# Two decode attentions in one kernel: how the last keys and the last values are split into transfers, and where the last output weights are reordered

## The chip, the cores and the metric

The kernel runs on one core of one Trainium2 chip. The metric is the device time of one execution in microseconds (us). Three executions of the kernel before took 1374.40, 1374.57 and 1374.70 us; the median is 1374.57.

## What is computed

Two attention layers decode one token for each of four batch rows; their outputs are put side by side. Layer A has 32 query heads that share 8 heads of keys and values, and looks at the last 2048 of 8192 positions. Layer B has 32 heads of its own and looks at all 8192 positions. All tensors are bf16, a head is 128 wide.

```python
def _A_ref(x, k_cache, v_cache, wq, wo):
    ...
    W = min(4096, max(256, Sk // 4))
    q = (x @ wq).reshape(B, Sq, Hq, Dh).transpose(0, 2, 1, 3)
    k = jnp.repeat(k_cache[:, :, Sk - W:, :], rep, axis=1)
    v = jnp.repeat(v_cache[:, :, Sk - W:, :], rep, axis=1)
    ...
def _B_ref(x, k_cache, v_cache, wq, wo):
    B, Sq, D = x.shape
    H, Dh = 32, 128
    q = (x @ wq).reshape(B, Sq, H, Dh).transpose(0, 2, 1, 3)
    scores = jnp.einsum("bhqd,bhkd->bhqk", q, k_cache) * (Dh ** -0.5)
    p = _softmax(scores, axis=-1)
    o = jnp.einsum("bhqk,bhkd->bhqd", p, v_cache)
    return o.transpose(0, 2, 1, 3).reshape(B, Sq, H * Dh) @ wo
...
return jnp.concatenate([a, b], axis=-1)
```

Almost all of the data is the key and value cache of layer B: 4 rows x 32 heads x 8192 positions x 128 x 2 bytes, 268 MB each for keys and values.

## The kernel before

**Chunks.** The caches are worked in chunks. A chunk of layer A is one shared head of all four rows (2 MB of keys, 2 MB of values). A chunk of layer B is two heads of one batch row: 128 tiles of 128 positions, 4 MB of keys and 4 MB of values, with each of the 128 partitions holding one contiguous run of 32 KB. There are 8 chunks of A (`NCA`) and 64 of B, 72 in all (`NC`); the last chunk is `NC - 1`.

**One chunk on the engines.** For each group of eight key tiles (`TG`), TensorE transposes the tiles into PSUM (`emit_T`), VectorE or ScalarE copies the result to SBUF (lines 475 and 477), and two groups later TensorE multiplies the transposed keys by the queries (`emit_S`). That is `keys_part`, 16 groups for a chunk of B. `values_part(c, nxt)` then runs the value product (`emit_pv`) of the chunk before while the softmax of the chunk just scored is worked out (row maximum, maximum over partitions, exponential). The value product of a chunk comes thus one chunk later than its scores. The last chunk has no successor: its value product stands at the end of the program, after line 806, followed by the division (`norm_out`), the output product (`emit_fin`) and the store.

**Order.** Nothing is scheduled automatically. The class `_Sched` records the operations of each engine in the order of the Python code, with the keys that an operation waits for; each key becomes a count of a semaphore, each engine's list is emitted in order, and the repeating part as a hardware loop.

**Loads.** All loads of caches and weights are issued by SyncE (SP) in one list (lines 375 to 398), each as one transfer of 128 partitions, and each waits until the buffer that it fills is free. The tensor `kv` has ten slots of 2 MB; B chunks use four of them for keys and four for values in turns of two, and the last values use slots 8 and 9, which hold layer A's keys earlier and are free early. So the last values can be issued before those of the chunk ahead of them are used. `dma_kv` issues them:

- the last keys in two pieces at lines 369 to 371: the first `LASTK` = 96 of 128 tiles (3 MB), then the other 32 (1 MB), with a semaphore of its own, `d_kl`;
- the last values in five pieces at lines 361 to 365, `LASTV` = 64, 32, 16, 8 and 8 tiles (2 MB, 1 MB, 512 KB, 256 KB, 256 KB), each with its own semaphore, `d_vl0` to `d_vl4`. `emit_pv` waits for a piece at its first tile (line 632).

**How waits for the second piece of the keys are made.** After the issue of the values of each odd chunk of B, SP waits for the output weights of B's current head pair (`wos`), in the last chunk also for `d_kl`, and then raises a count (line 394, keys `wos2`). TensorE waits for that count before the transposes of group `LASTK // TG` = 12 of every odd chunk of B (line 468), and before the output product (line 707), which `keys_part` puts after group 10. The transposes of the last chunk's group 12 so never start before the second piece of the keys is there.

**The last output weights.** `emit_fin` of the other chunks takes its left operand through `emit_sel`, which reorders the attention output. For the last chunk the weights are reordered instead, ahead of time: `emit_wol` (lines 686 to 696) multiplies them by constant selection matrices, four products of 512 columns into the PSUM tensor `tr`, and ScalarE and VectorE copy the two halves to `wol`. It stands after the first piece of the last value product, at line 810:

```python
for g in range(chunks[NC - 1]["NG"]):
    emit_pv(NC - 1, g)
    if g == LASTV[0] // TG - 1:
        emit_wol()
```

Of the kernel before, what the change touches and what calls it, by code (L numbers as in the profile page):

```python
# [12 lines left out]
P = 128  # L13
TG = 8
# [5 lines left out]
NSM = 2  # L20
SLAG = 2
NW = 64
LASTK = 96
LASTV = (64, 32, 16, 8, 8)

TRM0, BC0, L0, Q0, XT0 = 0, 256, 288, 320, 448
# [133 lines left out]
def bass_concat_heads__sliding_block_cached__mha_block_cached__decode_kernel(  # L160
# [31 lines left out]
    NCA = Hkv  # L192
# [8 lines left out]
    NTA, NTB = chunks[0]["NT"], chunks[-1]["NT"]  # L201
# [3 lines left out]
    sch = _Sched()  # L205
    with ExitStack() as es:
# [97 lines left out]
        def take(load, at, n, release):  # L304
            waits = []
            for i in range(at, at + n):
                waits += held[i]
                held[i] = [release]
            half_of[load] = at
            return waits  # L310

        def flat(at, n):
            return kv[:, at:at + n, :].rearrange("p s x -> p (s x)")
# [28 lines left out]
        def dma_kv(kind, c):  # L342
            ch = chunks[c]
            T = {("k", 0): A_k, ("k", 1): B_k, ("v", 0): A_v, ("v", 1): B_v}[(kind, ch["ab"])]

            at = HALF_A[kind][c % 2] if ch["ab"] == 0 else (0 if kind == "k" else 4) + 2 * (c % 2)

            if kind == "v" and c == NC - 1:
                at = 8
            waits = take((kind, c), at, 1 if ch["ab"] == 0 else 2, ("T", ch["s_last"]) if kind == "k" else ("pv", c))  # L350
            if kind == "v" and c == NCA + 1:
                waits = waits + [("pv", NONE)]
            if ch["ab"] == 0:
                src = T[:, ch["g"], SkA - W:, :].rearrange("b (pp j) d -> pp b (j d)", pp=P // NB)
                sch.add_dma("sp", lambda e: e.dma_start(kv[:, at, :], src), "d_h%d" % at, waits=waits, key=(kind, c))
                return
            src = T[ch["b"], 2 * ch["hp"]:2 * ch["hp"] + 2].rearrange("u (pp j) d -> (u pp) (j d)", pp=P // 2)
            dst = flat(at, 2)
            if kind == "v" and c == NC - 1:

                j0 = 0
                for i, n in enumerate(LASTV):
                    x = slice(j0 * P, (j0 + n) * P)
                    sch.add_dma("sp", lambda e, x=x: e.dma_start(dst[:, x], src[:, x]), "d_vl%d" % i, waits=waits, key=("vl", j0))
                    j0 += n
                return
            if kind == "k" and c == NC - 1:

                x = slice(0, LASTK * P), slice(LASTK * P, NTB * P)
                sch.add_dma("sp", lambda e: e.dma_start(dst[:, x[0]], src[:, x[0]]), "d_h%d" % at, waits=waits, key=(kind, c))  # L370
                sch.add_dma("sp", lambda e: e.dma_start(dst[:, x[1]], src[:, x[1]]), "d_kl", key="kl")
                return
            sch.add_dma("sp", lambda e: e.dma_start(dst, src), "d_h%d" % at, waits=waits, key=(kind, c))

        dma_x(0)
        dma_x(1)
        dma_wq(0, 0)
        dma_kv("k", 0)
        dma_wq(1, 6)

# [5 lines left out]
        for kind, c in loads:  # L386
            if kind == "k" and c >= NCA and (c == NCA or (c - NCA) % 4 == 3 and c > NCA + 3):
                dma_wos((c - NCA) // 4)
            dma_kv(kind, c)
            if kind == "v" and c > NCA and (c - NCA) % 2 == 1:  # L390


                hp = max(0, c - NCA - 2) // 4
                sch.add("sp", lambda e: e.sem_inc(sems["eng_sp"], 1), waits=[("wos", hp)] + (["kl"] if c == NC - 1 else []),
                        key=("wos2", c - 2 if c > NCA + 1 else NONE), self_inc=True)
            if kind == "v" and c < NCA:
                dma_wo(c)
# [7 lines left out]
        def pe_mm(o, l, r, start=True, stop=True, transpose=False, waits=(), key=None):  # L405
            if transpose:
                sch.add("pe", lambda e: e.transpose(o, l, r), waits, key)  # L407
            else:
                sch.add("pe", lambda e: e.matmul(o, l, r, start=start, stop=stop), waits, key)  # L409
# [37 lines left out]
        def tile_of(kind, c, j):  # L447
            at = half_of[(kind, c)]
            return flat(at, chunks[c]["NT"] // NTA)[:, j * P:(j + 1) * P]

        def ahead(c, n):

            return c - n if c - n >= NCA else NONE
# [3 lines left out]
        def emit_T(s):  # L457
            c, g = groups[s]
            bank = g % NTRB
            if c == NCA and g == 0:  # L460
                bank_used[:] = [None] * NTRB
            before, bank_used[bank] = bank_used[bank], s
            for t in range(TG):
                waits = []
                if t == 0:
                    waits = [("k", c), "c_identb"] if g == 0 else []
                    waits += [("ev", before)] if before is not None else []
                    if c >= NCA and c % 2 == 1 and g == LASTK // TG:
                        waits += [("wos2", ahead(c, 2))]
                pe_mm(tr[:, bank, t * P:(t + 1) * P], tile_of("k", c, g * TG + t), identb[:, :], transpose=True,  # L470
                      waits=waits, key=("T", s) if t == TG - 1 else None)
            src, dst = tr[:, bank, :], kt[:, s % NKT, :]
            waits = [("T", s)] + ([("S", s - NKT)] if s >= NKT else [])
            if (g % 3 == 2) if c >= NCA else (g in (0, 1, 3, 5)):
                sch.add("act", lambda e: e.activation(dst, src, ACTF.Copy), waits=waits, key=("ev", s))  # L475
            else:
                sch.add("dve", lambda e: e.tensor_copy(dst, src), waits=waits, key=("ev", s))  # L477
# [36 lines left out]
        def bcast(ap, dims):  # L514
            return bass.AP(ap.tensor, ap.offset, [ap.ap[0]] + dims)
# [122 lines left out]
        def norm_sum(c):  # L638
            if 0 <= c < NCA:
                m, n, rs, ri = c % NSM, 16, rst[0][:, c % NSM, :], rinv[:, c % NSM, :]  # L640
            else:
                m, n, rs, ri = NSM, 4, rst[1][:, :], rinv[:, 0, 0:4]
            pe_mm(ms[:, L0:L0 + n], onesf[:, :], rs, waits=([("rs", c), "c_onesf"] if c != NONE else []) + ms_read, key=("L", c))
            sch.add("dve", lambda e: e.reciprocal(out=ri, in_=ms[:, L0:L0 + n]), waits=[("L", c)], key=("rinv", c))
            if c >= NCA or c == NONE:

                pair = 4 * (c - NCA - 1 + 4) if c != NONE else 8
                pv = pm[:, :, :, :, :].rearrange("p a b c d -> p (a b c d)")
                sch.add("dve", lambda e, x=0: e.tensor_tensor(
                    out=rz[:, :].rearrange("p (x y) -> p x y", x=2), in0=bcast(ri, [[0, 2], [1, 4]]),  # L650
                    in1=pv[:, bass.ds(x + pair, 8)].rearrange("p (x y) -> p x y", x=2), op=ALU.mult),
                    waits=[("rinv", c), "c_pm"], key=("rz", c), at=pair)
            ms_read[:] = [("rinv", c)]
            rs_read[m] = [("L", c)]
# [31 lines left out]
        def emit_wol():  # L686

            for u in range(2):
                o = tr[:, u, :].bitcast(F32)
                for r in range(2):  # L690
                    pe_mm(o, back2[:, u, r, :], wos[:, r, :], start=r == 0, stop=r == 1,
                          waits=[("wos2", NC - 1)] if u == r == 0 else [], key=("back", u) if r else None)
                if u == 0:
                    sch.add("act", lambda e, o=o: e.activation(wol[:, 0, :], o, ACTF.Copy), waits=[("back", 0)], key=("wol", 0))
                else:
                    sch.add("dve", lambda e, o=o: e.tensor_copy(wol[:, 1, :], o), waits=[("back", 1)], key=("wol", 1))
# [26 lines left out]
        def pv_done(c):  # L723
            if c < NCA or (c - NCA) % 2:
                norm_out(c)
# [79 lines left out]
            values_part(None if c == 0 else NONE if c == NCA else c - 1, c)  # L805
        sch.mark()
        norm_sum(NC - 1)
        for g in range(chunks[NC - 1]["NG"]):
            emit_pv(NC - 1, g)
            if g == LASTV[0] // TG - 1:  # L810
                emit_wol()
        pv_done(NC - 1)
        emit_fin(NC - 1)

# [58 lines left out]
```

## Time and profile before

| what | value |
|---|---|
| time of the profiled execution | 1374.7 us |
| its span, first to last instruction | 1372.9 us |
| median of three runs | 1374.57 us |
| TensorE busy (PE) | 1181.3 us, 86% |
| its weight loads (PEld) | 1131.3 us, 82% |
| VectorE (DVE) | 657.2 us, 48% |
| ScalarE (ACT) | 434.8 us, 32% |
| mean granted TensorE clock | 0.939 |
| bytes read from HBM | 587.21 MB |
| keys of B, 63 loads of 4 MB | 27.1 us median from issue to landing |
| values of B, 63 loads of 4 MB | 31.4 us |
| last keys, 3 MB and 1 MB | 24.4 and 26.5 us |
| last values, 2 MB, 1 MB, 512 KB, 2 x 256 KB | 35.8, 37.8, 38.6, 38.7 us |

The engine names are those of the profile: PE is TensorE's matmul, PEld its weight load, SPq the instruction queue of SyncE, which issues the loads. L409 and L407 are the lines of one helper, `pe_mm`, through which all matmuls and transposes go, so they are told apart by their tiles: `tr<-identb,kv` are the transposes of keys, `sc<-qb,kt` the scores, `po<-pbb,kv` the value product, `tr<-wos,back` the reordering of the last output weights, `fin<-wol,oz` the last output product. "idle before <- releaser" behind an instruction tells how long its engine stood still and what ended that. "DMA share" is the mean busy share of the core's 16 DMA engines. A transfer's time from issue to landing includes the time that it lies behind earlier ones.

### The profile page before, as it was taken

What the parts mean: (1) busy time and instruction counts of PE and PEld (TensorE: products, weight loads), DVE (VectorE), ACT (ScalarE), POOL (GpSimd) and SP (SyncE); (2) the same over time, 40 slices, a digit from 0 to 9 for tenths busy, and PEclk for the clock granted to TensorE, in tenths of its full rate; (3) what the DMA queues carried; (4) which work ended last, traced back from release to release, by engine and by line L of the source; (5) the groups of instructions that cost most, each with busy time, mean ns of one, the idle gap of its engine ahead of it and who ended that gap; (6) DMA issues with size and microseconds to landing.
All of it is one profiled execution on the core that took longest, in us unless ns stands there. A gap on an engine that the chain in (4) does not pass through costs nothing.

```text
span 1372.9 us, 59836 instructions
## 1 busy us (share of the span) xinstructions
PE 1181.3 (86%) x27001; PEld 1131.3 (82%) x27001; DVE 657.2 (48%) x1434; ACT 434.8 (32%) x650; POOL 7.3 (1%) x28
## 2 busy tenths in 40 slices
PE   4898899888888988888899888888898888888988
PEld 4777898888888988888888878887888888888987
DVE  1775455444444544444445444444454444444544
ACT  1553233233233332333233323322333233223332
POOL 2000000000000000000000000000000000000000
PEclk9998999999999999999999999999999999999999
DMA  9999999999999999999999999999999999999998
GB/s 400 422 426 431 428 432 430 433 431 433 431 433 431 431 432 431 433 430 433 430 433 430 430 432 434 428 433 430 433 430 432 432 432 432 430 433 429 434 427 348
DMA packets 25253, 587.53 MB, mean 428 GB/s; under 512 B 2816, under 2 KB 2832, under 8 KB 6288
## 3 DMA queue, kind: packets, MB, share of 16 engines
q1 hardware_dynamic: 25208, 587.22, 99.7%
q8 instruction: 16, 0.26, 0.1%
q14 instruction: 5, 0.04, 0.0%
q10 hardware_dynamic: 24, 0.01, 0.0%
HBM read 587.21 MB, written 0.01 MB: 428 GB/s over the span
## 4 chain that ended last, share of the span: by engine, by line
DMA 59%; PE 37%; DVE 1%; issue 1%; ACT 1%; SPq 0%; DVEq 0%
DMA kv<-in_B_k_cache_dram 53%; PE tr L407 23%; PE sc L409 9%; DMA kv<-in_B_v_cache_dram 3%; PE po L409 2%; DMA kv<-in_B_wq_dram 2%; PE fin L409 2%; DMA kv<-in_A_k_cache_dram 1%; PE ms L409 1%; DVE sA L526 1%; ACT kt L475 0%; ACT pba L596 0%; DVE rm L535 0%; DVE sA L524 0%; PE ms L407 0%
## 5 line engine op out<-in xcount | busy, mean ns | idle before, releaser
L407 PE MATMUL tr<-identb,kv 128*128 128x128 bf16 x8704 | 697.4, 230 | 144.2 <-DMA kv<-in_B_k_cache_dram 139.5
L477 DVE COPY kt<-tr 128x1024 bf16<-128x1024 bf16 x736 | 502.9, 691 | 460.0 <-PE tr L407 455.6
L407 PEld LDWEIGHTS tr<-identb,kv 128*128 128x128 bf16 x8704 | 553.0, 104 | 166.9 <-DMA kv<-in_B_k_cache_dram 105.8
L475 ACT ACTIVATE kt<-tr 128x1024 bf16<-128x1024 bf16 x352 | 359.3, 1023 | 668.6 <-PE tr L407 668.3
L409 PE MATMUL sc<-qb,kt 128*128 128x64 bf16 x8704 | 444.8, 196 | 13.4 <-ACT kt L475 12.8
L409 PEld LDWEIGHTS sc<-qb,kt 128*128 128x128 bf16 x8704 | 364.9, 100 | 24.1 <-ACT kt L475 20.3
L409 PE MATMUL po<-pbb,kv 128*128 128x64 bf16 x8320 | 284.5, 192 | 5.3 <-issue 4.9
L409 PEld LDWEIGHTS po<-pbb,kv 128*128 128x128 bf16 x8320 | 263.3, 97 | 7.9 <-issue 5.1
L576 ACT ACTIVATE pbb<-sc,negb 64x128 bf16<-64x128 f32 x128 | 51.5, 403 | 252.4 <-DVE negb L563 251.6
L540 DVE TENSOR_REDUCE rm<-sc 64x1 f32<-64x128 f32 x128 | 37.0, 289 | 55.8 <-PE sc L409 55.0
L552 DVE TENSOR_REDUCE gm<-ms 1x2 f32<-1x128 f32 (+1 forms) x72 | 20.1, 279 | 47.8 <-PE ms L407 47.8
L563 DVE COPY negb<-ms 128x1 f32<-128x1 f32 (+1 forms) x72 | 11.4, 159 | 47.0 <-PE ms L409 47.0
L409 PE MATMUL ms<-identf,gx 1*128 1x1 f32 (+1 forms) x144 | 27.4, 257 | 0.8 <-DVE zA L682 0.8
L409 PEld LDWEIGHTS ms<-identf,gx 1*128 1x128 f32 (+1 forms) x144 | 21.3, 184 | 4.7 <-DVE zA L682 0.9
L665 DVE TENSOR_TENSOR oz<-po,rz 128x8 bf16<-128x8 f32 x33 | 5.5, 167 | 40.4 <-PE po L409 40.4
L576 ACT ACTIVATION_READ_ACCUMULATOR pbb<-sc,negb 64x1 f32 x128 | 23.7, 185 | 0.0
L407 PE MATMUL ms<-identf,rm 128*1 128x128 f32 (+1 forms) x72 | 19.6, 272 | 3.8 <-DVE rm L535 3.8
L409 PE MATMUL po<-pba,kv 128*128 128x64 bf16 x512 | 20.5, 199 | 2.6 <-ACT pba L596 1.4
L409 PEld LDWEIGHTS po<-pba,kv 128*128 128x128 bf16 x512 | 17.9, 102 | 5.4 <-ACT pba L596 4.2
L409 PE MATMUL fin<-wos,zB 128*4 128x512 bf16 x64 | 19.0, 378 | 0.0
L556 DVE TENSOR_SCALAR gx<-gm 1x128 f32<-1x128 f32 (+1 forms) x72 | 15.9, 221 | 2.5
L682 DVE CAST zB<-ms 64x8 bf16<-64x8 f32 x64 | 10.5, 164 | 8.9 <-PE ms L409 8.5
(61 smaller groups left out, 169.7 us busy)
## 6 DMA issues: line engine op xcount, KB each, us to landing
kv<-in_B_k_cache_dram SPq DMA_DIRECT2D x63, 4096.0 KB, 27.1
kv<-in_B_v_cache_dram SPq DMA_DIRECT2D x63, 4096.0 KB, 31.4
kv<-in_A_k_cache_dram SPq DMA_DIRECT2D x8, 2048.0 KB, 13.6
kv<-in_A_v_cache_dram SPq DMA_DIRECT2D x8, 2048.0 KB, 15.4
kv<-in_A_wq_dram SPq DMA_DIRECT2D x1, 4096.0 KB, 12.3
kv<-in_B_wq_dram SPq DMA_DIRECT2D x1, 4096.0 KB, 27.1
wor<-in_A_wo_dram SPq DMA_DIRECT2D x8, 512.0 KB, 9.5
wos<-in_B_wo_dram SPq DMA_DIRECT2D x16, 256.0 KB, 20.4
```

The costliest lines, as they stand in the source:

```text
L407: sch.add("pe", lambda e: e.transpose(o, l, r), waits, key)
L409: sch.add("pe", lambda e: e.matmul(o, l, r, start=start, stop=stop), waits, key)
L475: sch.add("act", lambda e: e.activation(dst, src, ACTF.Copy), waits=waits, key=("ev", s))
L477: sch.add("dve", lambda e: e.tensor_copy(dst, src), waits=waits, key=("ev", s))
L526: emit = lambda e, src=src, b=b: e.scalar_tensor_tensor(out=t, in0=src, scalar=mk[:, b:b + 1], in1=t, op0=ALU.mult, op1=ALU.add)
L540: sch.add("dve", lambda e, src=src, pp=pp: e.tensor_reduce(out=rm[pp, m, 0:1], in_=src, axis=AX.X, op=ALU.max), waits=[("S", ch["s_last"]) ...
L552: sch.add("dve", lambda e: e.tensor_reduce(out=gm[0:C, m, 0:U], in_=src, axis=AX.X, op=ALU.max), waits=[("trm", c)], key=("gmax", c))
L556: sch.add("dve", lambda e: e.tensor_scalar(out=dst, in0=gv, scalar1=-scale, scalar2=None, op0=ALU.mult), waits=[("gmax", c)], key=("gx", c))
L563: sch.add("dve", lambda e: e.tensor_copy(negb[:, m, 0:C], ms[:, col:col + C]), waits=[("bc", c)], key=("negb", c))
L576: sch.add("act", lambda e, src=src, pp=pp, n=n, u=u: e.activation(probs_of(c)[pp, :, u], src, ACTF.Exp, bias=negb[pp, m, 0:1], scale=scale ...
L665: sch.add("dve", lambda e: e.tensor_tensor(out=o, in0=i0, in1=i1, op=ALU.mult), waits=waits, key=("oT", c))
L682: sch.add("dve", lambda e, src=src, pp=pp: e.tensor_copy(z[pp, :].rearrange("p (r b) -> p r b", r=k), src), waits=[("sm", c)] + free if h ...
```

## The change

Three things change, all for the last chunk but for the position of one wait:

- the last keys come in two halves of 2 MB (64 tiles each), and the wait on the count of line 468 moves from group 12 to group 8 in every odd chunk of B; `LASTK` is gone;
- the four products and two copies of `emit_wol` are issued ahead of the last value product and not within it;
- the first 2 MB piece of the last values, one transfer of 128 partitions, becomes five transfers on the same semaphore: partitions 96 to 103, 104 to 111, 112 to 119 and 120 to 127, eight partitions of 16 KB each (128 KB a transfer), and then partitions 0 to 95 (1.5 MB). The key that the value product waits for is the count after all five.

The bytes loaded and the arithmetic are the same.

```diff
-LASTK = 96
 LASTV = (64, 32, 16, 8, 8)
...
                 for i, n in enumerate(LASTV):
                     x = slice(j0 * P, (j0 + n) * P)
-                    sch.add_dma("sp", lambda e, x=x: e.dma_start(dst[:, x], src[:, x]), "d_vl%d" % i, waits=waits, key=("vl", j0))
+                    if i == 0:
+
+                        for y in [slice(96 + 8 * k, 104 + 8 * k) for k in range(4)]:
+                            sch.add_dma("sp", lambda e, x=x, y=y: e.dma_start(dst[y, x], src[y, x]), "d_vl%d" % i, waits=waits)
+                        sch.add_dma("sp", lambda e, x=x: e.dma_start(dst[0:96, x], src[0:96, x]), "d_vl%d" % i, waits=waits, key=("vl", j0))
+                    else:
+                        sch.add_dma("sp", lambda e, x=x: e.dma_start(dst[:, x], src[:, x]), "d_vl%d" % i, waits=waits, key=("vl", j0))
                     j0 += n
                 return
             if kind == "k" and c == NC - 1:
 
-                x = slice(0, LASTK * P), slice(LASTK * P, NTB * P)
+                x = slice(0, NTB // 2 * P), slice(NTB // 2 * P, NTB * P)
...
-                    if c >= NCA and c % 2 == 1 and g == LASTK // TG:
+                    if c >= NCA and c % 2 == 1 and g == NTB // TG // 2:
                         waits += [("wos2", ahead(c, 2))]
...
         norm_sum(NC - 1)
+        emit_wol()
         for g in range(chunks[NC - 1]["NG"]):
             emit_pv(NC - 1, g)
-            if g == LASTV[0] // TG - 1:
-                emit_wol()
         pv_done(NC - 1)
```

## The prediction, made before the changed kernel ran

> **What bounds the kernel now.** I read the page's table of slices first, then its queue table, then the end of the chain of waits, then the timeline and the busy windows of the last 30 us. The profiled execution took 1374.7 us: a span of 1372.9 and 1.8 around it. The median of the runs shown, 1374.57, is 0.13 lower; the sum below is made against 1374.7.
>
> ```profile
> DMA  9999999999999999999999999999999999999998
> HBM read 587.21 MB, written 0.01 MB: 428 GB/s over the span
> q1 hardware_dynamic: 25208, 587.22, 99.7%
> q10 hardware_dynamic: 24, 0.01, 0.0%
> ```
>
> The load queue is busy 99.7% of the span. 428 GB/s over 16 engines is 26.8 GB/s for each, so a row of 16 KB takes 16384 / 26.8 = 0.61 us. The packet counts tell how transfers are split. The kernel issues 175 loads of 128 partitions and one store of four rows on q1: 175 x (128 + 16) + (4 + 4) = 25208, that is one packet a row and one small completion packet for each of 16 engines. On q10 there are three transfers of four rows, and 3 x (4 + 4) = 24: four rows go to four engines.
>
> ```profile
> 1330.42 38.58 DMA kv<-in_B_v_cache_dram
> 1369.04 0.42 PE po L409 x8
> 1369.56 0.18 DVE oz L665
> 1369.78 0.61 PE fin L409 x2
> 1370.41 0.68 DVE outsb L717
> ```
>
> The chain ends on the landing of the fifth piece of the last values at 1369.0; behind it lies a fixed tail of 3.9 us of span (eight tiles, the division, the output product, the store). What ends the program is when the slowest DMA engine has written its last row.
>
> ```profile
> core 0: us, PE busy (x) PEld busy (x) DVE busy (x) ACT busy (x) POOL busy (x), PEclk, DMA share, GB/s
> 1360.00:1365.00 5.00, 5.00 (x151) 4.87 (x148) 1.58 (x7) 0.91 (x4) 0.00 (x0) 1.00 0.98 405
> 1365.00:1366.00 1.00, 1.00 (x39) 1.00 (x35) 0.00 (x0) 0.00 (x0) 0.00 (x0) 1.00 0.67 268
> 1366.00:1367.00 1.00, 1.00 (x15) 0.53 (x12) 0.01 (x1) 0.45 (x1) 0.00 (x0) 1.00 0.56 223
> 1367.00:1368.00 1.00, 1.00 (x39) 1.00 (x36) 0.68 (x1) 0.15 (x1) 0.00 (x0) 1.00 0.52 193
> 1368.00:1369.00 1.00, 0.82 (x23) 0.58 (x18) 0.00 (x0) 0.00 (x0) 0.00 (x0) 1.00 0.11 43
> ```
>
> The DMA share falls from 1365 on: the engines don't end together. The completion packets in the trace's transfer records give it engine by engine (span time): seven end between 1365.4 and 1366.4, two near 1367.2, seven between 1368.6 and 1369.0. The idle shares after 1365 add to 0.33 + 0.44 + 0.48 + 0.89 = 2.1 us, which is all that a perfect spread could give, 0.16%.
>
> **The change, part by part.**
>
> ```profile
> 1328.21 7.75 SPq L364 DMA_DIRECT2D kv<-in_B_v_cache_dram  x5
> 1343.95 1.35 PE L409 MATMUL po<-pbb,kv 128*128 128x64 bf16 x40
> 1346.98 1.51 PE L407 MATMUL tr<-identb,kv 128*128 128x128 bf16 x24 [1.68 <-DMA kv<-in_B_k_cache_dram]
> 1359.15 0.65 PE L409 MATMUL po<-pbb,kv 128*128 128x64 bf16 x16 [0.23 <-DMA kv<-in_B_v_cache_dram]
> 1363.75 0.39 PE L409 MATMUL ms<-rsb,onesf 128*128 128x4 f32 x2
> 1364.04 1.93 PEld L409 LDWEIGHTS po<-pbb,kv 128*128 128x128 bf16 x64
> 1365.92 1.02 PE L409 MATMUL tr<-wos,back 128*128 128x512 bf16 x4
> 1366.78 2.04 PE L409 MATMUL po<-pbb,kv 128*128 128x64 bf16 x56
> ```
>
> *Last keys in halves.* The first piece shrinks from 3 MB, landing at 1346.9, to 2 MB: 1 MB at 428 GB/s is 2.4 us, so it lands at 1344.5. PE is free at 1343.95 + 1.35 = 1345.3, so the transposes start 1.7 us sooner. The second half still lands at 1322.86 + 26.5 = 1349.4, the bytes ahead of it being the same; the ninth group, which waits for it through the SP count, comes at 1352.0 - 1.7 = 1350.3, so no wait. But the values of the chunk before land at 1359.1 as now; PE reaches them at 1357.2, waits 1.9 in place of 0.23, and goes on at 1359.15. Worth 0. The cover is that landing; were it gone, the gain would be 1.7. The earlier wait on the SP count in every odd chunk (group 8 for 12) is met there: the trace has no PE wait on SP at all, and the product after group 10 waits for the same count now; the register instruction that it adds lies under the 139.5 us in which PE waits for keys of the second attention.
>
> *Output weights first.* Four products move from between the first 64 and the other 64 value tiles to ahead of them. They hold PE from 1365.92 to 1366.78, 0.86 us. They now run from 1364.04 to 1364.9, while the first piece is landing or late. PE's work to the end is the same: last eight tiles not before 1364.9 + 120 x 1.93/64 = 1368.5, against 1369.04 now. Worth 0 while the landing is later than that.
>
> *Nine issues for five on SP.* Four more issues at 0.43 us. The fifth of the present ones was held for 5.5 us (to 1336.0) with nine transfers outstanding. Behind them SP has the count that the ninth key group waits for. If the hold goes by rows outstanding, SP is free by 1338, far ahead of the keys at 1349.4. Worth 0; the other case is a rival.
>
> *The first 2 MB of values.* 128 rows in one transfer, eight rows an engine, 8 x 0.61 = 4.9 us, become 96 rows (six an engine) and four transfers of eight rows. By the packet counts an eight-row transfer goes to eight engines, a row each. The trace has none of 16 KB rows, so I bound its time t. Below: eight rows side by side, t = 0.61. Above: sixteen equal streams feed 128 partitions, so eight neighbouring partitions get one stream's worth in all loads of this kernel; if the 26.8 GB/s belongs to what is written into and not to the engine, the eight rows take 8 x 0.61 = 4.9. No row decides, since in the 128-partition loads engine and destination are always paired alike. The nearest is the first load of x, 4 KB into four partitions: in the transfer records its packets ran side by side within 97 ns, where one stream would need 152; that excludes the top for small packets, which may only have been buffered. I take the middle: two streams (four rows deep, 2.44), or one sharer more because the other engines still write there (five deep, 3.05); their mean, t = 2.75.
>
> The eight engines then spend 4t + 6 x 0.61 in place of 8 x 0.61, that is 4t - 1.22 more. If these are the engines that end early (the latest of them at 1367.3), the landing comes at 1367.3 + 4 x 2.75 - 1.22 = 1377.1, 8.1 after 1369.0. Sum: 1374.7 + 0 + 0 + 0 + 8.0 = **1382.7 us**. Four deep gives 1381.5, five deep 1384.0. The engines' order rests on the first four only: in the records the packets of the third four-row transfer lie in four of the eight streams that are ahead at that time (129 us).
>
> [...]
>
> [...]
>
> **The rivals.**
> - *The rows run side by side, on the early engines.* t = 0.61: the early eight end 1.22 later (1368.5 at most), the late ones 1.22 sooner (1367.8). PE then decides with 1368.5: 1374.7 - 0.5 = 1374.2. For it: the x packets, and 2.1 us of idle shares to be had. Against: a rate of 26.8 GB/s an engine that no load exceeds.
> - *The same, on the late engines or with no use:* 1369.0 + 1.22, so 1375.9. Against it: the four-row transfers on early streams.
> - *SP is held by transfers, not rows.* Each new issue waits until an older load is through: the ninth one then waits for the values before, landing until 1359.1, and the count for the ninth group comes at 1356 to 1359 in place of 1350.3. Slack is 1.9 (until 1352.2), then it decides: 4 to 7 us on PE, less about 1 us of waits there: 1377.5 to 1380.5. For it: the 5.5 us hold. Against: it ended at 1336.0, when the load under way was unfinished on nine engines.
> - *All eight rows in line:* t = 4.88, landing 1367.3 + 18.3 = 1385.6, so 1391.3.
>
> **How the numbers follow.** Shared writes, two to six deep (t 1.22 to 3.66; 1375.4 to 1386.4): 0.58, its own likely range 1378 to 1386.5. Side by side on the early engines, 1374.2: 0.24. On the late ones, 1375.9: 0.05. SP held: 0.06. In line: 0.07. 0.2% is 2.75 us, about what a measurement of this kernel can tell from no change. Faster by that is beyond the 2.1 us that idle engines leave: 0.02 for what I don't see. Within it are the second and third case and a little of the first (below three deep): 0.30. Slower: 0.68. The range, 1374.0 to 1386.0, leaves out the line-up and the ends.
>
> **What would show it.** The queue q1 should count 25208 + 32 = 25240 packets (4 x 16 + 112 for 144). Right, if 16 KB packets last over 1 us in the records where they last 0.61 now, the first piece lands near 1372 and the wait of PE before its first 64 value tiles is several us; the DMA share falls below 0.9 from 1356 on. Wrong, if packets stay at 0.61 and the share keeps above 0.9 until 1367: then it is the first rival. A PE wait at the ninth key group near 1350 would show the SP rival. Transposes of the last keys should start at 1345.3, and the output weights at 1364.0. The step I trust least is t.

## The result, and the profile after

The changed kernel takes 1386.2 us (median of 6 runs, 1385.28 to 1387.62) against 1374.43 for the kernel before (6 runs, 1374.17 to 1374.70): a ratio of 1.0086, 95% interval 1.0073 to 1.0099. It is slower by 11.8 us. The runs also scatter over 2.3 us, where those of the kernel before lie within 0.5. The profiled execution took 1386.49 us with a span of 1384.7.

The first lines are from the page of the changed kernel: its queue table and the table of slices.

```profile
PEclk9998999999999999999999999999999999999997
DMA  9999999999999999999999999999999999999997
GB/s 401 422 424 433 428 430 431 434 429 432 434 432 429 431 434 428 432 434 431 431 432 433 431 431 433 430 431 431 434 430 431 432 431 433 432 431 432 433 430 198
q1 hardware_dynamic: 25240, 587.22, 99.6%
```

The queue counts 25240 packets, 32 more than before, as worked out from eight rows and eight completions for each new transfer. All slices but the last are nearly as before; the last, 34.6 us long, moves 198 GB/s (348 before) while its DMA share still reads 7 tenths.

Next, the busy windows of the changed kernel at its end. The columns are the window, its length, busy time of PE, PEld, DVE, ACT and POOL, the granted clock, the DMA share and GB/s.

```profile
1350.00:1355.00 5.00, 5.00 (x112) 4.51 (x110) 3.31 (x8) 2.05 (x2) 0.00 (x0) 1.00 1.01 423
1355.00:1360.00 5.00, 1.95 (x47) 1.71 (x43) 1.38 (x3) 1.02 (x1) 0.00 (x0) 1.00 1.02 233
1360.00:1365.00 5.00, 2.61 (x49) 2.61 (x50) 0.58 (x2) 0.00 (x0) 0.00 (x0) 0.52 0.95 193
1365.00:1370.00 5.00, 5.00 (x100) 4.44 (x97) 1.00 (x5) 0.96 (x5) 0.00 (x0) 0.80 0.95 200
1370.00:1375.00 5.00, 0.58 (x7) 0.23 (x6) 0.69 (x1) 0.55 (x1) 0.00 (x0) 0.88 0.92 220
1375.00:1380.00 5.00, 5.00 (x99) 5.00 (x97) 0.00 (x0) 0.00 (x0) 0.00 (x0) 0.50 0.29 111
```

This is the reading to learn from. From 1355 to 1375 the DMA engines are busy 92% of the time or more, and they move 193 to 233 GB/s, about half of the 423 just before. The busy share is the time that packets take, so packets that are held up look like work (those of 16 KB took 1.22 us in the mean, 0.61 before); GB/s beside it shows that something is wrong. The clock column falls to 0.52 and 0.50 in the windows that come with PE's waits of 5.24 and 4.42 us.

The timeline of PE in the changed kernel, with the waits that ended there (L412 and L414 are the lines of `pe_mm` here; in the experiments its lines shift by a few):

```profile
1345.22 1.50 PE L412 MATMUL tr<-identb,kv 128*128 128x128 bf16 x24
1350.26 0.61 PE L412 MATMUL tr<-identb,kv 128*128 128x128 bf16 x8
1362.39 1.04 PE L414 MATMUL po<-pbb,kv 128*128 128x64 bf16 x16 [5.24 <-DMA kv<-in_B_v_cache_dram]
1369.32 1.02 PE L414 MATMUL tr<-wos,back 128*128 128x512 bf16 x4
1374.77 6.57 PE L414 MATMUL po<-pbb,kv 128*128 128x64 bf16 x128 [4.42 <-DMA kv<-in_B_v_cache_dram]
```

Transposes of the last keys start at 1345.22 and the ninth group goes at 1350.26 without a wait. The values of the chunk ahead now land at 1362.4, 3.2 us later than in the kernel before (1359.15). The first piece of the last values lands at 1374.7 where PE found it at 1364.04. Then all 128 tiles run in one stretch of 6.57 us with no wait for the four later pieces. The chain of waits of the changed kernel says the same:

```profile
1331.18 43.54 DMA kv<-in_B_v_cache_dram
1374.73 0.04 issue
1374.77 6.58 PE po L414 x128
```

The sum closes: the first piece is 10.7 us later (1374.73 - 1364.04). From there to the end of the value product it takes 6.6 us, where the kernel before took 5.4 (1364.04 to 1369.47): 1.2 more. That is 11.9 us, and the span grew by 11.8. Read from the other end: the last piece lands at 1379.5 in this trace (1369.0 before), 10.5 later, and what follows it takes 5.3 us in place of 3.9, as PE is still busy with earlier tiles.

The transfer records (one line a packet) give the time of a packet, by size, after 1350 us of span. "Added" is the time over the usual one, summed and divided by 16 engines.

| packet | usual | changed kernel, mean | added per engine |
|---|---|---|---|
| 32 KB, values of the chunk ahead | 1.22 us | 1.44 us | 1.30 us |
| 16 KB, first piece | 0.61 us | 1.22 us | 4.87 us |
| 8 KB, second piece | 0.31 us | 0.58 us | 2.15 us |
| 4 KB, third piece | 0.16 us | 0.24 us | 0.63 us |
| 2 KB, fourth and fifth | 0.085 us | 0.10 us | 0.26 us |

Not one of the 128 16 KB packets of the first piece took over 0.622 us in the kernel before. In the changed kernel the slowest took 1.64, and 32 KB packets of the chunk ahead took up to 2.65. Packets of loads that the change doesn't touch are slow too: those of the second piece took 0.58 us in place of 0.31.

### The profile page after: what moved, and what is told of

Same layout as the page of the kernel before. It is cut to its first block, busy times and chain, and to the rows that moved or that the text cites. A ratio compares the mean times of both kernels' runs of the same rounds, so it can differ in the third digit from the quotient of the medians.

```text
span 1384.7 us, 59840 instructions
## 1 busy us (share of the span) xinstructions
PE 1184.2 (86%) x27001; PEld 1133.5 (82%) x27001; DVE 656.6 (47%) x1434; ACT 435.1 (31%) x650; POOL 7.4 (1%) x28
## 3 DMA queue, kind: packets, MB, share of 16 engines
q1 hardware_dynamic: 25240, 587.22, 99.6%
## 4 chain that ended last, share of the span: by engine, by line
DMA 62%; PE 36%; issue 1%; DVE 1%; ACT 1%; SPq 0%; DVEq 0%
DMA kv<-in_B_k_cache_dram 53%; PE tr L412 22%; PE sc L414 9%; DMA kv<-in_B_v_cache_dram 3%; DMA kv<-in_A_k_cache_dram 3%; PE po L414 3%; DMA kv<-in_B_wq_dram 2%; PE fin L414 2%; PE ms L414 1%; ACT kt L480 0%; DVE sA L531 0%; ACT pba L601 0%; PE ms L412 0%; DVE zA L687 0%; SPq L366 0%
## 5 line engine op out<-in xcount | busy, mean ns | idle before, releaser
L412 PE MATMUL tr<-identb,kv 128*128 128x128 bf16 x8704 | 694.1, 230 | 143.3 <-DMA kv<-in_B_k_cache_dram 136.0
L412 PEld LDWEIGHTS tr<-identb,kv 128*128 128x128 bf16 x8704 | 549.3, 104 | 166.1 <-DMA kv<-in_B_k_cache_dram 97.5
L414 PE MATMUL sc<-qb,kt 128*128 128x64 bf16 x8704 | 446.4, 196 | 14.7 <-ACT kt L480 12.8
L414 PEld LDWEIGHTS sc<-qb,kt 128*128 128x128 bf16 x8704 | 366.0, 100 | 26.4 <-ACT kt L480 20.2
L414 PE MATMUL po<-pbb,kv 128*128 128x64 bf16 x8320 | 288.7, 193 | 14.6 <-DMA kv<-in_B_v_cache_dram 9.7
L414 PEld LDWEIGHTS po<-pbb,kv 128*128 128x128 bf16 x8320 | 267.8, 98 | 17.2 <-DMA kv<-in_B_v_cache_dram 10.3
L414 PE MATMUL ms<-identf,gx 1*128 1x1 f32 (+1 forms) x144 | 27.2, 256 | 0.8 <-DVE zA L687 0.8
L414 PEld LDWEIGHTS ms<-identf,gx 1*128 1x128 f32 (+1 forms) x144 | 21.1, 182 | 4.6 <-DVE zA L687 0.9
L414 PE MATMUL po<-pba,kv 128*128 128x64 bf16 x512 | 20.5, 199 | 2.6 <-ACT pba L601 1.4
L414 PEld LDWEIGHTS po<-pba,kv 128*128 128x128 bf16 x512 | 17.9, 102 | 5.4 <-ACT pba L601 4.2
L412 PE MATMUL ms<-identf,rm 128*1 128x128 f32 (+1 forms) x72 | 19.7, 273 | 2.7 <-DVE rm L540 2.7
L414 PE MATMUL fin<-wos,zB 128*4 128x512 bf16 x64 | 19.0, 378 | 0.0
L687 DVE CAST zB<-ms 64x8 bf16<-64x8 f32 x64 | 10.5, 164 | 9.4 <-PE ms L414 8.9
```

The costliest lines, as they stand in the source:

```text
L687: sch.add("dve", lambda e, src=src, pp=pp: e.tensor_copy(z[pp, :].rearrange("p (r b) -> p r b", r=k), src), waits=[("sm", c)] + free if h ...
```

## The experiments

Three theories were held against each other, each a supposition for the runs to test. P: the partitions written decide; a row keeps the usual rate where its engine writes the block of partitions that it writes in a load of 128, and is slow where it meets other engines. (Which partitions an engine writes stands in no record.) S: a transfer of eight rows has a price of its own. B: only the bytes per engine count. A fourth, H, puts the cost on the reading side of memory. Every run was compared with runs of the kernel before on the same chip.

**one_transfer: keys and output weights as changed, no split.**

```diff
-                    if i == 0:
...
+                    sch.add_dma("sp", lambda e, x=x: e.dma_start(dst[:, x], src[:, x]), "d_vl%d" % i, waits=waits, key=("vl", j0))
```

> The changed kernel with the first piece of the last values as one transfer of 128 partitions again; keys in halves and output weights first stay. If the split alone costs (both theories of it): 1374.4 us as before, within 0.5, packets of 16 KB rows at 0.61 us, transposes of the last keys starting about 1.7 us earlier than before against the landing of the values ahead, and PE waiting about 2 us for those. If the keys or the output weights carry part of the cost: 1375 to 1386 us.

Measured: 1374.83 us against 1374.60, ratio 1.0003 (0.9993 to 1.0012). The keys in halves and the moved output weights change nothing that the runs can tell. Its PE timeline shows where the head start goes:

```profile
1345.00 1.50 PE L406 MATMUL tr<-identb,kv 128*128 128x128 bf16 x24
...
1359.01 0.65 PE L408 MATMUL po<-pbb,kv 128*128 128x64 bf16 x16 [2.08 <-DMA kv<-in_B_v_cache_dram]
...
1363.86 1.02 PE L408 MATMUL tr<-wos,back 128*128 128x512 bf16 x4
1364.72 3.94 PE L408 MATMUL po<-pbb,kv 128*128 128x64 bf16 x120
1368.88 0.41 PE L408 MATMUL po<-pbb,kv 128*128 128x64 bf16 x8 [0.23 <-DMA kv<-in_B_v_cache_dram]
```

The transposes start 2.0 us sooner than in the kernel before, and the wait for the values ahead grows from 0.23 to 2.08 us. The output weights fill the time before the first 120 tiles, and the last eight still wait for the landing.

**split_only: the kernel before with nothing but the split.** Its edit is the part of the diff of `dma_kv` that begins with `if i == 0`, put into the kernel before.

> The kernel before with the split of the first piece alone: keys in three and one quarters and output weights within the value product stay. If the split is the whole cost: 1386 us, within the scatter of the changed kernel (1385.3 to 1387.6), perhaps 0.3 to 0.9 us more, as the four products of the output weights then come after the late landing. If keys in halves carry part of it: 1375 to 1384 us.

Measured: 1387.03 us against 1374.49, ratio 1.0090 (1.0073 to 1.0106). With the run before it, the whole cost is in the split.

**rows32_rows96: one transfer of 32 rows in place of four of eight.**

```diff
-                        for y in [slice(96 + 8 * k, 104 + 8 * k) for k in range(4)]:
+                        for y in [slice(96, 128)]:
```

> The first piece as two transfers: partitions 96 to 127 (32 rows, two an engine, so every engine has its eight rows again and no engine has more bytes than another) and 0 to 95. Theory P: still slow, since 96 rows at six an engine put the engines out of step with the blocks of partitions: rows over 1 us, end at 1379 to 1384 us. Theory S (transfers of eight rows are the cost): 1374.4 to 1375.5. Theory B: 1374.4.

Measured: 1383.6 us against 1374.6, ratio 1.0069 (1.0052 to 1.0086). By its queue's 25224 packets both transfers run on 16 engines, so all have the same bytes again, and no transfer has eight rows, yet the kernel is 9.0 us slower than before. B and S can't explain that. The 16 KB packets take 1.22 us here as well. The windows, first of the kernel before, then of this run, show the halved rate, 229 and 206 GB/s in place of 406:

```profile
1355.00:1360.00 5.00, 4.57 (x116) 4.33 (x114) 2.06 (x3) 2.05 (x2) 0.00 (x0) 1.00 0.95 406
```

```profile
1355.00:1360.00 5.00, 1.98 (x48) 1.74 (x43) 1.40 (x3) 1.02 (x1) 0.00 (x0) 0.88 0.99 229
1360.00:1365.00 5.00, 2.46 (x47) 2.47 (x48) 0.58 (x2) 0.00 (x0) 0.00 (x0) 0.50 1.00 206
```

**The cost by itself.** For the next runs the first piece is one transfer of 128 partitions again, as in one_transfer. Ahead of it stand four extra transfers of eight rows of 12 KB (0.39 MB) into `wor`, the buffer of layer A's output weights, which nobody reads any more. Only the partitions that are written or read differ from run to run.

*extra_neighbours:*

```diff
+                for y in [slice(8 * k, 8 * k + 8) for k in range(4)]:
+                    sch.add_dma("sp", lambda e, y=y: e.dma_start(wor[y, :, :].rearrange("p a b -> p (a b)"), src[y, 0:NWO * 4 * DO]), "d_ex", waits=waits + [("fin", NCA - 1)])
...
+            e.wait_ge(sems["d_ex"], 64)
```

> One transfer of 128 partitions for the first piece, and ahead of it four extra transfers of eight neighbouring partitions (0 to 7, 8 to 15, 16 to 23, 24 to 31), 12 KB a row, into a buffer that nobody reads any more: 0.39 MB more loaded, nothing of the outputs touched. A row of 12 KB takes 0.46 us at the usual rate, four of them 1.8 us on the engines that end 1.7 to 3.6 us early. [...] Theory S (a transfer of eight rows has a price of its own, whatever partitions it writes): the same time as the run with stepped partitions. Theory B (only the share of bytes per engine counts): 1374.4 to 1374.8.

*extra_stepped:* `slice(k, 32, 4)` in place of `slice(8 * k, 8 * k + 8)`.

> The same four extra transfers, same bytes and same count of rows, but each to partitions 0, 4, 8 ... 28 (then 1, 5 ... and so on), so that the eight rows of a transfer lie in eight different blocks of four. Theory P: rows take 0.46 us, as in the loads of 128 partitions, and the end is 1374.4 to 1374.8 us. Theory S: as slow as with neighbouring partitions. Theory B: 1374.4 to 1374.8, also with neighbours.

*extra_other_half:* `slice(64 + k, 96, 4)`.

> [...] Theory S: as with stepped partitions 0 to 31. Theory B: 1374.4 to 1374.8.

*dst32_stepped:* written to `wor[32 + k:64:4]`, read from `src[k:32:4]`.

> As with stepped partitions, but written to 32, 36 ... 60 (then 33, 37 ...). [...]

*src0_dst64:* written to `wor[64 + k:96:4]`, read from `src[k:32:4]`.

> As the run with extra transfers to the other half (partitions 64, 68 ... 92 and so on), but read from the rows that the run with stepped partitions read (0, 4 ... 28 and so on); what they load is used by nobody. If what is written into decides (theory P): rows of 12 KB at 0.8 to 0.95 us and 1379 to 1381 us, as with the other half. If the rows that are read decide (theory H): 0.46 us and 1376 us, as with stepped partitions.

*src64_dst0:* written to `wor[k:32:4]`, read from `src[64 + k:96:4]`.

> The counterpart: read from rows 64, 68 ... 92 and so on, written to partitions 0, 4 ... 28 and so on. Theory P: rows at 0.46 us, 1375.8 to 1376.7 us. Theory H: 0.8 to 0.95 us, 1379 to 1381 us.

Measured; "12 KB" and "16 KB" are the mean times of one packet, usually 0.46 and 0.61 us:

| run | read from rows | written to partitions | 12 KB | 16 KB | time | before | ratio (95%) |
|---|---|---|---|---|---|---|---|
| extra_neighbours | 0-7, 8-15 ... | the same | 0.75 | 0.80 | 1379.83 | 1374.60 | 1.0039 (1.0025 to 1.0054) |
| extra_stepped | 0, 4 ... 28 ... | the same | 0.46 | 0.61 | 1376.14 | 1374.60 | 1.0011 (1.0002 to 1.0021) |
| extra_other_half | 64, 68 ... 92 ... | the same | 0.86 | 0.85 | 1380.17 | 1374.49 | 1.0042 (1.0028 to 1.0057) |
| dst32_stepped | 0, 4 ... 28 ... | 32, 36 ... 60 ... | 0.46 | 0.61 | 1376.05 | 1374.55 | 1.0010 (1.0001 to 1.0020) |
| src0_dst64 | 0, 4 ... 28 ... | 64, 68 ... 92 ... | 0.86 | 0.90 | 1380.33 | 1374.55 | 1.0041 (1.0027 to 1.0055) |
| src64_dst0 | 64, 68 ... 92 ... | 0, 4 ... 28 ... | 0.46 | 0.61 | 1375.99 | 1374.55 | 1.0010 (1.0001 to 1.0020) |

All six load the same bytes with the same number of transfers, rows and engines. The last two are the sharpest pair: what is read and what is written are exchanged, and the time follows the partitions that are written. With extra_stepped and extra_other_half they make all four pairings of these two groups of rows and partitions. For these eight-row transfers H falls, S falls (a transfer of eight rows runs at the full rate in three of the six), and B falls. What is left is P, as far as the partitions written decide; the prices below are not what shared writes alone would give. The windows of that pair, first src0_dst64, then src64_dst0:

```profile
1355.00:1360.00 5.00, 4.50 (x93) 3.82 (x90) 2.62 (x4) 2.05 (x2) 0.00 (x0) 1.00 1.02 234
```

```profile
1355.00:1360.00 5.00, 4.28 (x111) 4.05 (x109) 2.06 (x3) 2.05 (x2) 0.00 (x0) 1.00 0.93 394
```

234 against 394 GB/s, with the DMA share the other way round, 1.02 against 0.93.

What the extras cost was missed. The well placed extras were expected at 1374.4 to 1374.8 by P and B alike, since the early engines have 1.7 us and more to spare, and cost 1.5 us. No packet in that run is slow. But in its records, where rows can be followed because each starts when the one before it on its engine ends, the last of the engines that take extra rows starts its four at 1358.3, when the last row of the values ahead has only 0.4 us left (1358.65). At least one of the eight is thus hardly early, and its four rows of 0.46 us, less 0.4, are the 1.5 us. The extras to the other half cost 5.7 us. Were their own rows alone slow, an estimate from the table gives 4 x (0.86 - 0.46) = 1.6 us more than extra_stepped; it is 4.0 more, as the rows of the 128-partition load that follows are slow as well (0.85 us in the mean). And four rows deep, as in the prediction's middle, the rows of extra_neighbours would take 4 x 0.46 = 1.8 us, an estimate. They took 0.75 in the mean and 0.93 at most, and still the end is at 1379.83: a lower price on the extra rows, and again one on the rows beside and behind them.

**split_stepped: the four transfers of the change, rows four apart.**

```diff
-                        for y in [slice(96 + 8 * k, 104 + 8 * k) for k in range(4)]:
+                        for y in [slice(96 + k, 128, 4) for k in range(4)]:
```

> The changed kernel with the four transfers of eight rows to partitions 96, 100 ... 124, then 97, 101 ... and so on: eight different blocks of four in each. Bytes, engines, transfers and the 96-row transfer as in the changed kernel. [...] Theory S: 1386 as the changed kernel. Theory H (the cost is on the reading side of memory, by rows that don't follow each other): slower than the changed kernel.

Measured: 1384.89 us against 1374.49, ratio 1.0073 (1.0056 to 1.0090). That is 1.3 us less than the changed kernel by the medians, with ranges that meet at 1385.28. The 128 packets of 16 KB took 1.18 us in the mean (1.22 in the changed kernel), so placing the eight-row transfers otherwise changes little. The run speaks against H, which had it slower, and with so small a difference does not tell P from S.

**kept_busy: the changed kernel with PE kept at work while it waits.**

```diff
+        for _ in range(140):
+            pe_mm(sc[:, 0, 0:NW], identb[:, :], qb[:, 0, 0:NW])
         for g in range(chunks[NC - 1]["NG"]):
```

> The changed kernel with 140 matmuls of 64 columns into scores that nobody reads any more, between the output weights and the wait for the first piece; they leave the outputs as they are. PE waits there 4.4 us, and the 128 value tiles after it take 6.58 us at a granted clock of 0.5, where 128 tiles took 3.9 us in the profile of before. If the idle time is what lowers the clock: the tiles go back to some 0.030 us each and the end comes with the landing of the last piece near 1380.0 of span, 0.5 to 1.2 us sooner than the changed kernel (1385.3 or so, scatter of 1 us either way). If the clock falls for another reason: same time, tiles at 0.05 us.

Measured: 1385.34 us (1385.07 to 1386.49) against 1374.49, 0.9 below the median of the changed kernel, though the ranges overlap. The timeline is clearer than the times:

```profile
1370.85 4.25 PE L414 MATMUL sc<-qb,identb 128*128 128x64 bf16 x140
1375.26 2.05 PE L414 MATMUL po<-pbb,kv 128*128 128x64 bf16 x64 [0.16 <-DMA kv<-in_B_v_cache_dram]
1377.48 2.30 PE L414 MATMUL po<-pbb,kv 128*128 128x64 bf16 x56 [0.18 <-DMA kv<-in_B_v_cache_dram]
1380.01 0.41 PE L414 MATMUL po<-pbb,kv 128*128 128x64 bf16 x8 [0.23 <-DMA kv<-in_B_v_cache_dram]
```

64 tiles take 2.05 us as in the kernel before, 0.032 us each, and the last eight wait for their landing. In the changed kernel 128 tiles took 6.57 us, 0.051 each, at a granted clock of 0.50 after 4.4 us of waiting. The slow tiles come from that idle time. Here the last piece lands at 1379.97 and 3.9 us follow, as in the kernel before; in the profiled execution of the changed kernel it landed at 1379.5 and 5.3 us followed. The slow tiles cost 1.4 us there, and 0.9 of the 11.8 by the medians.

No run beats the kernel before.

## Why the prediction was right and wrong

*Right in direction, and in what decides.* It named shared writes as the likeliest case (0.58), and the pairs of runs above show that the partitions written decide for eight-row transfers (0.46 us against 0.86 for the same rows read). The measured 1386.2 lies 3.5 above the 1382.7 forecast and 0.2 above the range.

*Last keys in halves, worth 0:* right, also in its parts. Transposes at 1345.22 (forecast 1345.3), ninth group at 1350.26 with no wait (1350.3), and a wait of 2.08 us for the values ahead in one_transfer (1.9).

*Output weights first, worth 0:* right, by the same run.

*Nine issues on SP, worth 0:* right. The last four issues of the changed kernel are through by 1336.3, with four more transfers outstanding than before, so the number of transfers alone doesn't set the hold, and that rival falls.

```profile
1331.55 4.79 SPq L369 DMA_DIRECT2D kv<-in_B_v_cache_dram  x4
```

*The step that failed* is the term "4t + 6 x 0.61" with t = 2.75. No run shows that t, a middle taken between bounds, nor the two streams behind it. The term put all of the price on four transfers, left the other rows at 0.61 and stopped at the first piece. The records show the reverse. The rows of the eight-row transfers took about 1.2 us each, so t was 1.2. But the 96 rows, six an engine, took 1.25 each in place of 0.61, and the table above has 1.3 us added in the values ahead and 3.0 in the later pieces. An estimate with these means: the eight engines spend 4 x 1.2 + 6 x 1.25 in place of 4.9, that is 7.4 more, and 1.3 + 3.0 beside it, 11.7 in all where the term gave 9.8. The last piece landed at 1379.5, and the forecast was 1377.1. rows32_rows96 shows that a split into 32 and 96 rows costs 9.0 us without any eight-row transfer. By P, 96 rows at six an engine are out of step with the loads of 128 partitions; that this is what slows them was the author's supposition, carried over from the eight-row runs. No run shows which partitions an engine writes, and none places 96 rows otherwise.

That the forecast came as near as 3.5 us is partly luck. With t = 1.2 and the rest of its sum as it stands it would have been 1376.6: a price too high on four rows stood in for one on rows that it left at 0.61.

*A term was put at nothing:* the clock. The 3.9 us after the landing were taken as fixed and measured 5.3, as PE's wait of 4.4 us left it at a granted clock of 0.50; kept_busy has 3.9 again. With the landing 2.4 us later than forecast, these 1.4 us make up the 3.8 by which the profiled execution, 1386.49, lies above the forecast.

*Signs and sums.* Packets over 1 us and a PE wait of several us came as forecast; the DMA share below 0.9 from 1356 on did not, it stayed at 0.92 to 1.02 until 1375. By the prediction's own sum the low end of its first case, t = 1.22, is 1376.7 and not 1375.4.

*The first rival* (1374.2, chance 0.24) needed both full rate and early engines. Neither held: the rows were slow, and where extra rows did run at full rate (extra_stepped), they made the end 1.5 us later, as at least one of the eight engines is nearly the last. So the sum's condition, that these eight end by 1367.3, did not hold either.

*What shared writes don't account for.* By dst32_stepped, partitions 32 to 63 are as free for these engines as 0 to 31 (0.46 us in both), while rows to 64 to 95 are slow (0.86). In extra_neighbours the 0.93 at most is about what two rows deep give, 2 x 0.46, and half of four deep; its rows start anywhere between 1354.9 and 1362.8, so whether four were ever under way side by side is not shown. And in that run, which adds rows in 0 to 31 alone, 24 of the 32 KB packets of the values ahead took over 1.4 us and up to 2.62, and among them are rows of up to 2.15 us on engines that take none of the extra rows. Nothing in the runs says what those would share with the extra rows.

*Left open:* why rows of the untouched loads are slow as well, beside and behind the rows placed otherwise (0.80 to 0.90 us in place of 0.61), and why most slow rows take 1.6 to 2 times as long, on engines with extra rows and without. How the writes go was not seen; that they are shared is inferred from which partitions are slow.

## What to carry to other kernels

Where a kernel runs at the DMA limit, as this one does with its load queue busy 99.7% of the span, don't cut a load by partitions to move bytes between DMA engines: here it halved the rate of the load queue for 20 us (193 to 233 GB/s in place of 423), and loads that nobody had touched became slow with it (8 KB packets 0.58 us in place of 0.31). Cut along the row, and keep 128 partitions: so cut, the last values of the kernel before ran at the usual rate (16 KB in 0.61 us, 8 KB in 0.31, 4 KB in 0.16). Read GB/s beside the DMA share, as the share alone stayed at 0.92 to 1.02 through the worst of it; and before bytes are moved to engines that seem early, check with a small extra load which engines it really uses: in extra_stepped at least one of them was ahead by only 0.4 us.

## What the runs showed of the hardware that was not expected

- Eight-row transfers ran at full rate (12 KB in 0.46 us, none over 0.469) with their rows four partitions apart in the first or second 32 (extra_stepped, src64_dst0, dst32_stepped), and at about half (0.86 us) with the same rows written to partitions 64 to 95 (src0_dst64).
- Slow rows took 1.6 to 2 times as long in the mean: 0.75 us for extra_neighbours and 0.86 for extra_other_half against 0.46, 1.22 against 0.61 in the changed kernel.
- It spread: the mean 16 KB packet of an untouched 128-partition load behind slow extra rows took 0.80 to 0.90 us (extra_neighbours, extra_other_half, src0_dst64), 0.61 behind the others.
- With waits of 5.24 and 4.42 us PE's granted clock fell to 0.52 and 0.50 in the changed kernel, and 128 tiles took 6.57 us in place of about 4.1; with PE kept at work (kept_busy) the clock stayed at 1.00 from 1375 to 1380 and 64 tiles took 2.05.
